# LayerNorm of the first chunk in pairs of blocks, and the first Q and K spreads in more and smaller loads, in a fused attention + gated-MLP kernel

## The chip, the cores and the metric

One core of one Trainium2 chip. The metric is the device time of one execution in microseconds; the kernel before was run five times. A profile of one execution gives the times of the single instructions.

## The reference

For x of 2048 rows and 640 columns, the layer adds attention and a gated MLP, both computed from one LayerNorm, to x:

```python
xn = _layernorm(x, axis=-1)                     # no weight, eps 1e-5
# attention: 32 heads of 20, each row sees itself and the 255 rows before it
qkv = (xn @ wqkv).reshape(1, 2048, 3, 32, 20)
scores = q @ k.T * 20 ** -0.5;  p = softmax(masked scores)
A = (p @ v) @ wo
# gated MLP, hidden width 1536
B = (sigmoid(xn @ w_gate) * (xn @ w_up)) @ w_down
return x + A + B
```

(The lines of attention are put together from the reference's own, batch and transposes left out.)

## The kernel before

The 2048 rows are worked in four chunks of 512, and a chunk in four blocks of 128 rows. For a chunk:

- **LayerNorm.** `ln_block` (L191 to L201) takes the statistics of a block on VectorE (`bn_stats` L195 twice, `bn_aggr` L197) and 1/sqrt on GpSimd (L199, L200, tile `rstd`). `norm_block` (L205) makes `xn` on VectorE. `transpose_block` (L213) turns a block with five TensorE transposes into a PSUM tile `pt`, which ScalarE (chunk 0, L216) or VectorE (later chunks, L218) copies to `xnT`, rows along the free dimension.
- **V.** `proj_v` makes a block's V: ten matmuls (L260) in two halves, each copied out to `v` (L264; on ScalarE for chunk 0). GpSimd first sets the extra columns of `v` (L255, L256).
- **Q and K.** `proj_block` makes a fifth of Q or K of a chunk: five matmuls (L234, tile `pqk`), a cast to `st` (Q on VectorE L238, K on ScalarE L240), and a store of 128 KB from `st` to a scratch in HBM (`sq`, `sk`, L242). `spread` (L249) loads Q or K back from the scratch, so that heads lie at 32-row steps: tile `qT` or `kT`, eight groups of four heads, 128 KB for each group. Each group needs rows of all five stores.
- **Scores and output.** `scores` (L394 matmuls into `ps`, L400 exp on ScalarE to `pT`, L405 and L409 masks on GpSimd) goes in three steps for each group of heads; `pv` (L420) multiplies by V, and `finish_group` (L430 on, VectorE) divides.
- **MLP.** `g_gu`: gate (L319, `pg`), tanh on ScalarE (L322, `th`), up (L326, `pu`), and the product on VectorE (L330, `h`). `down` (L345) and `outp` (L358, L363) finish a block with the output projection and the residual x.

The order on every engine is the order in which the program emits instructions, and that is written out by hand. All loads are issued by SyncE (SP) except x of block 1, which ScalarE issues, and one half of the last block's output. SyncE issues in program order, so a transfer that waits for a store holds up those behind it.

The start runs so: x of chunk 0 in four loads by block, with the V part of the QKV weights in between (L135 to L140), the Q and K parts, the first halves of the gate and up weights (L153), and zeros for the scratch (L149). Then LayerNorm, transposes and V of chunk 0; then Q and K of chunk 0 (`g_qk(0)`), then `load_rest`: the second halves of the gate and up weights, x of chunk 1 (L118, tile `xc`), the zeros of the second scratch, `wd` and `wo`. The order of LayerNorm and V in chunk 0 is the loop at L486:

```python
    stat = {0: ln_block(0, 0)}
    for s in range(SBC + 1):
        if s + 1 < SBC:
            stat[s + 1] = ln_block(0, s + 1)
        if s < SBC:
            norm_block(0, s, *stat[s])
            transpose_block(0, s, True)
        if s:
            proj_v(0, s - 1)
```

After that a loop (L529) emits the steps of `scores` for all chunks and groups and, between them, "fill" work of TensorE, by credit: gate and up of chunk 0 first, six such tiles ahead of the first scores (L525). From the tenth piece of that fill on, LayerNorm of chunk 1 (`g_norms(1)`) is mixed in, so its statistics stand in VectorE's order among the `h` of chunk 0.

PSUM buffers: `pt`, `pv`, `pqk`, `pg`, `pu` share three (`ps_d`); `ps` has two of two banks (`ps_s`), `acc` one. Five buffers of `st`, four of `pT`, two of `th`.

Of the kernel before, what the change touches and what calls it, by code (L numbers as in the profile page):

```python
# [18 lines left out]
SBC = CW // P  # L19
HG = 4  # L20
NG = H // HG
# [49 lines left out]
def kernel(  # L71
# [119 lines left out]
    def ln_block(c, s):  # L191
        xs = xc[c][:, s, :]
        stats = lnp.tile([P, 2, nc.vector.BN_STATS_DIM], FP32, name="stats")
        for a in range(2):
            nc.vector.bn_stats(out=stats[:, a, :], in_=xs[:, a * 320:(a + 1) * 320])  # L195
        mv = lnp.tile([P, nc.vector.BN_AGGR_DIM], FP32, name="mv")
        nc.vector.bn_aggr(out=mv, in_=stats)  # L197
        rstd = lnp.tile([P, 1], FP32, name="rstd")
        nc.gpsimd.tensor_scalar(out=rstd, in0=mv[:, 1:2], scalar1=EPS, scalar2=None, op0=ADD)  # L199
        nc.gpsimd.tensor_tensor(out=rstd, in0=rstd, in1=neghalf, op=POW)  # L200
        return mv, rstd  # L201

    def norm_block(c, s, mv, rstd):
        xn = lnp.tile([P, D], BF16, name="xn", bufs=4)
        nc.vector.tensor_scalar(out=xn, in0=xc[c][:, s, :], scalar1=mv[:, 0:1],  # L205
                                scalar2=rstd[:, 0:1], op0=SUB, op1=MULT)
        xns[c, s] = xn

    def transpose_block(c, s, act):
        xn = xns.pop((c, s))  # L210
        pt = ps_d.tile([P, DC, P], BF16, name="pt", tag="d")
        for d in range(DC):
            nc.tensor.transpose(pt[:, d, :], xn[:, d * P:(d + 1) * P], ident)  # L213
        dst = xnT[c][:, :, s * P:(s + 1) * P]
        if act:
            nc.scalar.copy(out=dst, in_=pt)  # L216
        else:
            nc.vector.tensor_copy(out=dst, in_=pt)  # L218

    def new_xnT(c):  # L220
        xnT[c] = xtp.tile([P, DC, CW], BF16, name="xnT")
# [5 lines left out]
    def proj_block(w, c, m):  # L227


        base = 0 if w == "q" else D  # L230
        ps = ps_d.tile([P, CW], FP32, name="pqk", tag="d")
        for d in range(DC):
            wt = wqkv[:, d, base:base + D].rearrange("p (k m) -> p m k", m=DC)
            nc.tensor.matmul(ps, lhsT=wt[:, m, :], rhs=xnT[c][:, d, :],  # L234
                             start=(d == 0), stop=(d == DC - 1))
        st = stp.tile([P, CW], BF16, name="st")
        if w == "q":
            nc.vector.tensor_copy(out=st, in_=ps)  # L238
        else:
            nc.scalar.copy(out=st, in_=ps)  # L240
        dst = scratch[w, c % 2].rearrange("(h j) s -> h j s", j=32)
        nc.sync.dma_start(out=dst[:, 4 * m:4 * m + 4, :], in_=st)  # L242

    def spread(w, c, g0, g1):

        if g0 == 0:
            qk[w, c] = (qp if w == "q" else kp).tile([P, NG, CW], BF16, name=w + "T")
        src = scratch[w, c % 2].rearrange("(g p) s -> p g s", p=P)
        nc.sync.dma_start(out=qk[w, c][:, g0:g1, :], in_=src[:, g0:g1, :])  # L249

    def proj_v(c, s):
        v = vp.tile([P, H * VW + 11], BF16, name="v")
        vt[c * SBC + s] = v
        v3 = v[:, 0:H * VW].rearrange("p (h d) -> p h d", d=VW)
        nc.gpsimd.memset(v3[:, :, DH:VW], 0.5)  # L255
        nc.gpsimd.memset(v[:, H * VW:], 0.0)  # L256
        for hf in range(2):
            ps = ps_d.tile([P, CW], FP32, name="pv", tag="d")
            for d in range(DC):
                nc.tensor.matmul(ps[:, 0:HALF], lhsT=xnT[c][:, d, s * P:(s + 1) * P],  # L260
                                 rhs=wqkv[:, d, 2 * D + hf * HALF:2 * D + (hf + 1) * HALF],
                                 start=(d == 0), stop=(d == DC - 1))
            copy = nc.vector.tensor_copy if c else nc.scalar.copy
            copy(out=v3[:, hf * 16:(hf + 1) * 16, 0:DH],  # L264
                 in_=ps[:, 0:HALF].rearrange("p (h d) -> p h d", d=DH))
# [24 lines left out]
    def g_qk(c):  # L290
        for w in "qk":
            for m in range(DC):
                proj_block(w, c, m)
                if w == "k" and m == 1:
                    spread("q", c, 0, NG)
                yield 5 * MM
        if c == 0:
            spread("k", c, 0, 1)
            spread("k", c, 1, NG)

    def g_v(c):
        for s in range(SBC):
# [179 lines left out]
            yield cost  # L482

    new_xnT(0)
    stat = {0: ln_block(0, 0)}
    for s in range(SBC + 1):  # L486
        if s + 1 < SBC:
            stat[s + 1] = ln_block(0, s + 1)
        if s < SBC:
            norm_block(0, s, *stat[s])  # L490
            transpose_block(0, s, True)
        if s:
            proj_v(0, s - 1)
    for _ in g_qk(0):
        pass
    load_rest()
# [7 lines left out]

    fill.add("gu0", mix(g_gu(0, 0, 12), chain(g_norms(1), g_transposes(1)), 9), 12 * GU + 1280)
    fill.add("qk1", mix(g_qk(1), g_norms(2), 2), 50 * MM)
    fill.add("v1", g_v(1), 40 * 136)
    fill.add("gu1a", g_gu(1, 0, 1), 1 * GU)
    fill.add("out0", mix(g_out(0), g_transposes(2), 1, 3), OUT + 1280)
    fill.add("x3", later(3), 0)  # L510
    fill.add("qk2", g_qk(2), 50 * MM)
    fill.add("v2", g_v(2), 40 * 136)
    fill.add("gu1b", mix(g_gu(1, 1, 12), g_norms(3), 10), 11 * GU)
# [31 lines left out]
    c = NCH - 1  # L545
# [46 lines left out]
```

## Time and profile before

| | us |
|---|---|
| five runs, median (lowest to highest) | 335.84 (334.18 to 337.28) |
| the profiled execution | 334.18 |
| its span, first to last instruction | 332.4 |
| TensorE matmul busy | 320.0 |
| ScalarE busy | 218.2 |
| GpSimd busy | 165.0 |
| VectorE busy | 163.4 |
| granted TensorE clock | 1.00 |

The profiled execution was the quickest of the five runs. The page says what each engine was busy with; a matmul counts as busy while it streams, and the ends of matmuls are modelled. Where the time goes is read from the stretches in which TensorE is idle: 12.4 us in the span. Of the first 60 us the engines look like this (busy us in the stretch, DMA rate):

| stretch | TensorE | VectorE | ScalarE | GpSimd | DMA GB/s |
|---|---|---|---|---|---|
| 6 to 8 | 0.78 | 1.73 | 0.69 | 1.07 | 370 |
| 8 to 14 (three of 2) | 6.00 | 1.79 | 4.62 | 2.12 | 368 to 372 |
| 30 to 32 | 1.60 | 0.53 | 0.60 | 0.00 | 66 |
| 32 to 34 | 1.46 | 0.39 | 1.09 | 0.00 | 219 |
| 34 to 40 (three of 2) | 6.00 | 1.38 | 5.03 | 2.78 | 373 to 376 |
| 40 to 44 (two of 2) | 2.93 | 0.80 | 2.49 | 0.89 | 364 to 406 |

### The profile page before, as it was taken

The page shows a single profiled execution, that of the slowest core. Times are in us where ns is not written, and L with a number is a line of the kernel's source. Part 1 is how long each engine was busy: PE and PEld are TensorE (multiplying, and loading weights), DVE is VectorE, ACT ScalarE, POOL GpSimd, SP SyncE. Part 2 cuts the span into 40 slices and gives each one's busy share as a digit, 9 for nine tenths or more (in the row PEclk, how much of TensorE's full clock was granted, in tenths as well). Part 3 has the DMA queues.
Part 4 walks back from the last instruction along what each step waited for, and adds up shares of the span by engine and source line. Part 5 has one row for each costly group of instructions (what it writes and reads, how often), then busy time and mean ns, then how long its engine had stood idle before and what let it go on. Part 6 is the DMA issues. An engine that isn't in the chain of part 4 may idle for free.

```text
span 332.4 us, 7219 instructions
## 1 busy us (share of the span) xinstructions
PE 320.0 (96%) x2884; PEld 165.0 (50%) x2884; DVE 163.4 (49%) x333; ACT 218.2 (66%) x274; POOL 165.0 (50%) x312
## 2 busy tenths in 40 slices
PE   7998979989899999999999999999999999999996
PEld 2653323445466655544455654544445664444664
DVE  5232177698654363636954445443443425444142
ACT  2623776769666568788875667868887657878300
POOL 5200457576655554664954455565455554554300
PEclk9999999999999999999999999999999999999999
DMA  8956997125501044700000012630000010000001
GB/s 271 376 183 196 373 390 224 35 81 156 177 0 42 22 130 130 238 17 3 0 2 22 20 41 81 205 128 4 0 2 1 26 37 20 2 0 2 2 17 62
DMA packets 26224, 30.89 MB, mean 93 GB/s; under 512 B 1456, under 2 KB 25648, under 8 KB 26160
## 3 DMA queue, kind: packets, MB, share of 16 engines
q1 hardware_dynamic: 25904, 30.20, 27.5%
q8 instruction: 22, 0.36, 0.5%
q10 hardware_dynamic: 288, 0.25, 0.2%
q14 instruction: 10, 0.08, 0.1%
HBM read 21.00 MB, written 10.26 MB: 94 GB/s over the span
## 4 chain that ended last, share of the span: by engine, by line
PE 84%; DMA 6%; ACT 3%; DVE 3%; POOL 1%; SPq 1%; issue 1%; ACTq 0%; POOLq 0%
PE y L345 16%; PE pqk L234 14%; PE pu L326 13%; PE pg L319 13%; PE ps L394 9%; PE y L358 7%; PE acc L420 6%; PE pv L260 6%; DMA xc<-in_A_x_dram 5%; ACT pT L400 3%; DMA sk<-st 1%; PE pt L213 1%; DVE stats L195 1%; DVE t L430 0%; POOL pT L405 0%
## 5 line engine op out<-in xcount | busy, mean ns | idle before, releaser
L400 ACT ACTIVATE pT<-ps 128x1024 bf16<-128x1024 f32 (+2 forms) x192 | 175.9, 971 | 61.8 <-PE ps L394 58.0
L405 POOL TENSOR_SCALAR_AFFINE_SELECT pT<-pT 128x512 bf16<-128x512 bf16 x128 | 81.7, 638 | 79.8 <-ACT pT L400 79.6
L409 POOL TENSOR_SCALAR_AFFINE_SELECT pT<-pT 128x512 bf16<-128x512 bf16 x112 | 71.8, 641 | 58.1 <-ACT pT L400 58.1
L330 DVE SCALAR_TENSOR_TENSOR h<-th,pu 128x512 bf16<-128x512 f32 x48 | 32.7, 682 | 59.9 <-PE pu L326 21.3
L319 PE MATMUL pg<-xnT,wg 128*128 128x512 bf16 x240 | 59.8, 380 | 1.0 <-DVE h L330 1.0
L326 PE MATMUL pu<-xnT,wu 128*128 128x512 bf16 x240 | 59.9, 380 | 0.0
L345 PE MATMUL y<-wd,h 128*128 128x320 bf16 x384 | 57.3, 300 | 0.0
L234 PE MATMUL pqk<-xnT,wqkv 128*128 128x512 bf16 x200 | 46.6, 381 | 0.0
L394 PE MATMUL ps<-qT,kT 20*128 20x384 bf16 (+2 forms) x704 | 39.6, 275 | 5.2 <-ACT pT L400 4.2
L345 PEld LDWEIGHTS <-h 128*128 128x128 bf16 x384 | 35.7, 98 | 16.8 <-issue 4.0
L322 ACT ACTIVATE th<-pg 128x512 f32<-128x512 f32 x48 | 28.8, 600 | 13.9 <-PE pg L319 13.3
L430 DVE STREAM_TRANSPOSE t<-acc 128x512 f32<-128x512 f32 x32 | 22.8, 713 | 28.5 <-PE acc L420 28.1
L319 PEld LDWEIGHTS <-wg 128*128 128x128 bf16 x240 | 22.1, 98 | 28.3 <-issue 4.5
L326 PEld LDWEIGHTS <-wu 128*128 128x128 bf16 x240 | 21.3, 98 | 27.0 <-issue 5.2
L234 PEld LDWEIGHTS <-wqkv 128*128 128x128 bf16 x200 | 22.3, 119 | 19.3 <-issue 2.9
L363 DVE SCALAR_TENSOR_TENSOR y_sb<-y,xc 128x320 bf16<-128x320 f32 x32 | 15.4, 490 | 32.6 <-PE y L358 32.6
L394 PEld LDWEIGHTS <-kT 20*128 20x128 bf16 x704 | 12.3, 92 | 37.0 <-issue 35.3
L420 PE MATMUL acc<-pT,v 128*32 128x384 bf16 (+2 forms) x704 | 25.7, 277 | 0.2 <-POOL pT L405 0.2
L260 PE MATMUL pv<-wqkv,xnT 128*128 128x320 bf16 x160 | 23.9, 299 | 0.4 <-DVE v L264 0.4
L358 PE MATMUL y<-wo,oc 128*128 128x320 bf16 x160 | 24.1, 299 | 0.0
L420 PEld LDWEIGHTS <-v 128*32 128x32 bf16 x704 | 15.0, 96 | 13.6 <-issue 11.0
L238 DVE CAST st<-pqk 128x512 bf16<-128x512 f32 x20 | 13.8, 688 | 12.5 <-PE pqk L234 10.8
(32 smaller groups left out, 175.4 us busy)
## 6 DMA issues: line engine op xcount, KB each, us to landing
qT<-sq SPq DMA_DIRECT2D x4, 1024.0 KB, 6.0
kT<-sk SPq DMA_DIRECT2D x3, 1024.0 KB, 5.3
sq<-st SPq DMA_DIRECT2D x20, 128.0 KB, 2.2
sk<-st SPq DMA_DIRECT2D x20, 128.0 KB, 3.0
wqkv<-in_A_wqkv_dram SPq DMA_DIRECT2D x3, 800.0 KB, 5.7
out_dram<-y_sb SPq DMA_DIRECT2D x15, 160.0 KB, 1.8
wg<-in_B_w_gate_dram SPq DMA_DIRECT2D x2, 960.0 KB
wu<-in_B_w_up_dram SPq DMA_DIRECT2D x2, 960.0 KB
```

Source lines behind the costliest of these rows:

```text
L234: nc.tensor.matmul(ps, lhsT=wt[:, m, :], rhs=xnT[c][:, d, :], start=(d == 0), stop=(d == DC - 1))
L260: nc.tensor.matmul(ps[:, 0:HALF], lhsT=xnT[c][:, d, s * P:(s + 1) * P], rhs=wqkv[:, d, 2 * D + hf * HALF:2 * D + (hf + 1) * HALF], start=( ...
L319: nc.tensor.matmul(pg, lhsT=part(wg, d, f), rhs=xnT[c][:, d, :], start=(d == 0), stop=(d == DC - 1))
L326: nc.tensor.matmul(pu, lhsT=part(wu, d, f), rhs=xnT[c][:, d, :], start=(d == 0), stop=(d == DC - 1))
L330: nc.vector.scalar_tensor_tensor(out=h, in0=th, scalar=1.0, in1=pu, op0=ADD, op1=MULT)
L345: nc.tensor.matmul(ys[hf], lhsT=ht[c, f][:, s * P:(s + 1) * P], rhs=wd[:, f, hf * HALF:(hf + 1) * HALF], start=(f == 0), stop=False)
L358: nc.tensor.matmul(ys[hf], lhsT=oc[c, m][:, s * P:(s + 1) * P], rhs=wo[:, m, hf * HALF:(hf + 1) * HALF], start=False, stop=(m == DC - 1))
L394: nc.tensor.matmul(pss[i // 2][:, i % 2, col * P:(col + n) * P], lhsT=qk["k", kc][32 * i:32 * i + DH, g, kb * P:(kb + 1) * P], rhs=qk["q", ...
L400: nc.scalar.activation(out=pt[:, 2 * a:2 * a + 2, 0:width * P], in_=pss[a][:, :, 0:width * P], func=EXP, scale=SCALE)
L405: nc.gpsimd.affine_select(out=v, in_=v, pattern=[[0, HG], [1, P]], compare_op=GE, fill=0.0, base=0, channel_multiplier=-1)
L409: nc.gpsimd.affine_select(out=v, in_=v, pattern=[[0, HG], [-1, P]], compare_op=GE, fill=0.0, base=-1, channel_multiplier=1)
L420: nc.tensor.matmul(acc[32 * i:32 * i + 32, q0 * P:(q0 + n) * P], lhsT=v[:, h * VW:h * VW + 32], rhs=pt[:, i, col * P:(col + n) * P], start ...
```

## The change

LayerNorm of chunk 0 goes in two pairs: statistics of two blocks, then normalisation and transposes of both, then V of both. The load of Q of chunk 0, which was one of 1,024 KB, becomes one of groups 0 and 1 (256 KB) at the same place and one of groups 2 to 7 (768 KB) behind K's second load. The load of K, which was group 0 (128 KB) and groups 1 to 7 (896 KB), becomes group 0, groups 1 and 2 (256 KB) and, behind the second of Q, groups 3 to 7 (640 KB). Later chunks are as before. Lines from L301 on move down by two.

```diff
             for m in range(DC):
                 proj_block(w, c, m)
                 if w == "k" and m == 1:
-                    spread("q", c, 0, NG)
+                    spread("q", c, 0, NG if c else 2)
                 yield 5 * MM
         if c == 0:
             spread("k", c, 0, 1)
-            spread("k", c, 1, NG)
+            spread("k", c, 1, 3)
+            spread("q", c, 2, NG)
+            spread("k", c, 3, NG)
...
     new_xnT(0)
-    stat = {0: ln_block(0, 0)}
-    for s in range(SBC + 1):
-        if s + 1 < SBC:
-            stat[s + 1] = ln_block(0, s + 1)
-        if s < SBC:
-            norm_block(0, s, *stat[s])
+    for s0 in range(0, SBC, 2):
+        stat = [ln_block(0, s) for s in (s0, s0 + 1)]
+        for s in (s0, s0 + 1):
+            norm_block(0, s, *stat[s - s0])
             transpose_block(0, s, True)
-        if s:
-            proj_v(0, s - 1)
+        for s in (s0, s0 + 1):
+            proj_v(0, s)
     for _ in g_qk(0):
         pass
     load_rest()
```

## The prediction

> **What bounds the kernel now.** I read the chain that ended last first, then its pieces in order of time over the first 60 us, where all of the change lies.
>
> ```profile
> PE 84%; DMA 6%; ACT 3%; DVE 3%; POOL 1%; SPq 1%; issue 1%; ACTq 0%; POOLq 0%
> PE y L345 16%; PE pqk L234 14%; PE pu L326 13%; PE pg L319 13%; PE ps L394 9%; PE y L358 7%; PE acc L420 6%; PE pv L260 6%; DMA xc<-in_A_x_dram 5%; ACT pT L400 3%; DMA sk<-st 1%; PE pt L213 1%; DVE stats L195 1%; DVE t L430 0%; POOL pT L405 0%
> ```
>
> TensorE carries the span: 320.0 us busy of 332.4, so 12.4 us idle in all, and no edit that leaves the matmuls alone can win more. The transfers in the chain are two: the loads of x, 5%, and the stores of K, 1%. The pieces of the chain say where:
>
> ```profile
> 14.33 10.81 PE pqk L234 x50
> 25.16 0.59 ACT st L240
> 25.77 4.51 DMA sk<-st
> ...
> 30.75 0.44 SPq L249
> 31.23 0.56 SPq L153
> 31.83 0.53 SPq L153
> 32.41 10.78 DMA xc<-in_A_x_dram
> 43.20 0.90 DVE stats L195 x2
> 44.34 0.76 DVE stats L195 x2
> 45.25 0.64 DVE h L330
> ```
>
> Columns: start and length in us, then what. The path does not run through the first scores. It goes from the last store of K (25.77, landed 30.28) through SyncE's queue (the K loads, gate and up weights) to the load of x of chunk 1, which lands at 43.2; LayerNorm of chunk 1 stands ahead of an h in VectorE's order, and TensorE then needs that h. The list of waits over the span and over 30 to 56 us prices the stops (total, times, longest, us):
>
> ```profile
> PE pt L213 <- DVE xn L205: 1.2, 1, 1.2
> PE ps L394 <- DMA kT<-sk: 0.9, 1, 0.9
> PE pg L319 <- DVE h L330: 1.0, 2, 0.7
> DVE stats L195 <- DMA xc<-in_A_x_dram: 4.3, 1, 4.3
> ```
>
> The change aims at the first two rows. The timeline shows that the last two stand behind them: the h of 45.25 us is for a pu whose matmuls began at 39.40; it waits behind the statistics, and pg at 45.94 needs its PSUM buffer.
>
> **What the Trainium skill says.** "DMA: Bandwidth & Descriptors", Anatomy of one DMA, puts a fixed 2.0 us on each transfer, most of it the receipt of the last write. The trace agrees: Q stores of the later chunks land in 2.0 us (minimum and median). The same page, Two DMAs through the same engine are not ordered, has a dependent load wait for the completion of the store; SyncE's issue of the K load waits up to 3.7 us here. Specifications there give 358 to 368 GB/s; here 34 to 43 us moved 376. "SBUF — State Buffer", Who interferes with whom, says that VectorE in a two-port mode and GpSimd block each other. The trace fits: xn takes 394 to 450 ns, but 646 ns at 9.95 us, amid GpSimd's memsets of v.
>
> **Part 1, LayerNorm in pairs.** No instruction is added. Four orders change.
> VectorE: xn of block 1 goes ahead of the statistics of block 2 (6.39 to 7.44). It now waits for rstd, ready at 6.84. GpSimd's four memsets of v of blocks 0 and 1 stand right behind that rstd, so xn takes 0.39 to 0.65 and ends at 7.25 to 7.5. T1, the five transposes, starts at 7.29 to 7.55 instead of 7.89: 0.34 to 0.60 of the 1.2 us wait goes.
> TensorE: before, T0 T1 V0 T2 V1 T3 V2 V3 (V: a block's ten V matmuls); after, T0 T1 V0 V1 T2 T3 V2 V3. V1 used to cover the copy of block 2 to xnT on ScalarE; now only T3 does. T1 at 7.55, V0 0.29 later, V0 and V1 2.72 (four halves of 0.68), so T2 at 10.55 and TensorE free at 11.12. The copy begins about 0.5 after T2's start (9.54 to 10.06 before), behind V1's last 0.43 us eviction, and takes 0.70: V2 at 11.8, a new stall of 0.68. V2 and V3 end 2.72 later, at 14.52, against 14.17 before, when pqk L234 began. With the quick xn: 14.26. So this part costs 0.09 to 0.35; I take **+0.2**.
> xn of block 3 comes at about 10.5 to 11.1: T3 can slip a few tenths inside the stall. GpSimd's memsets pass ahead of rstd of blocks 2 and 3, which wait for statistics anyway; ScalarE's evictions of V1 pass ahead of that copy, counted above. All of it shifts K's last store, and so x of chunk 1, by as much.
>
> **Part 2, smaller loads.** SyncE issues two more L249 loads, at 0.34 to 0.44 each: 0.8 us ahead of the gate weights. In the stretch 23.6 to 26.3 (KB each, median us to landing), with a later chunk's Q stores (minimum, median, maximum) below:
>
> ```profile
> qT<-sq SPq DMA_DIRECT2D x1, 1024.0 KB, 6.0
> sk<-st SPq DMA_DIRECT2D x3, 128.0 KB, 5.3
> ...
> DMA to landing us min/median/max: 2.0/2.0/3.6
> ```
>
> The Q load (issued 23.28, landed 29.3) stands ahead of the last three K stores, whose last took 4.51 instead of 2 to 3. With 256 KB in place of 1,024, 768 KB (786 kB) leave the way, 2.3 us at 26 to 28 us' 340 GB/s. The last store then lands about 1.0 after that Q load, as before, or 2.0 to 3.0 after issue: 28.0 to 28.8, taken 28.3. K's first load is issued 2.0 us earlier and takes 2.15 (30.36 to 32.5 before): 30.5. First scores follow the gate and up matmuls that end at 31.6, so the **0.94 us wait goes**. 0.2 from part 1 leaves that unchanged. Groups 0 and 1 have Q and K by about 31.5; group 1's scores ran at 39.1. The rest of both lands by about 36; group 2's scores ran at 47.1. No wait is added at TensorE.
>
> But the 768 KB of Q and the K loads stand ahead of x of chunk 1, and that queue is full:
>
> ```profile
> 30.00:31.00 1.00, 1.00 (x6) 0.42 (x5) 0.24 (x1) 0.44 (x1) 0.00 (x0) 1.00 0.00 0
> 34.00:43.00 9.00, 7.94 (x63) 3.17 (x61) 1.38 (x2) 6.99 (x12) 3.67 (x6) 1.00 1.07 376
> ```
>
> The last two columns are DMA share and GB/s: empty at 30, saturated from 34 to 43. Starting 2.05 earlier and carrying 786 kB more at 376 GB/s (2.09) cancel: x lands at 43.2 + 0.05, plus part 1's 0.2. Unknown is the ramp after an issue (2 to 3 us below full rate here): bounds -0.6, if short loads in flight together fill it, and +2.1, if the store lands no earlier. SyncE's issues have room: x's would come at 31 to 32, before at 32.41. The counters of completion, reused in turn every eight transfers, now make the second gate load wait for the first Q load and a K clear for K's first load: both landed by then.
>
> TensorE thus arrives about 0.75 us earlier at the pg that waits for h, and h still waits for x: the 0.36 us stop there grows to about 1.1, and what follows starts where it did, plus x's delay. **Late next is x of chunk 1.**
>
> **Sum.** Part 1 +0.2; K wait -0.94, given back at h +0.94; x +0.05, rounded with the two transfers' own gaps to +0.1. Total +0.3 on the profiled execution's 334.18 (span 332.4). That execution was the quickest of five, 1.66 below their median; on 335.84 this gives **336.1**.
>
> **Rivals.** A, the gain is kept: x lands 0.9 or more earlier, because the half-empty stretches (144 GB/s at 24 to 26, 0 at 30, 66 at 30 to 32) are filled. Net -0.94 + 0.2 = -0.7: 335.1. For it: that empty microsecond. Against: in the new order the same stretch still only waits for K's store. For more than 1% (3.4 us), nearly all waits of TensorE before 56 us (1.2 + 0.9 + 1.4 at ScalarE's exp + 1.0 at h) would have to vanish.
> B, slower: K's last store keeps its 4.5 us since writing, not the Q load, holds it. Then K's first load is no earlier, the 0.94 stays, and x waits behind 786 kB more: +2.1 + 0.2, **338.1**. It decides from the point where the store gains less than 2.1 us. For it: the first Q store, with no Q load ahead, took 3.9. Against: that one followed the clears, and all three K stores landed just after Q. Past 1% it needs x 3.4 us late, so further contention.
> C, the split does nothing because scores wait for the whole tile: before, the first scores began 1.8 us after the issue of the 896 KB K load, which needs 2.4 at 376 GB/s, so they wait for their own piece. That leaves little for C.
>
> **How the numbers follow.** Forecast 0.60, A 0.16, B 0.19, others (C and shifts of later stages) 0.05. 1% is about what a measurement of this kernel tells from no change (its runs span 334.18 to 337.28). The forecast itself lies within 1%, A mostly and B too, B with a tail beyond: faster 0.07, same 0.80, slower 0.13. The range takes in A's 335.1 less a microsecond of run spread and B's 338.1 with half of one: 334.1 to 338.6.
>
> **What would show it.** Part 1: T1 near 7.4, a gap of about 0.6 before V2, pqk at 14.2 to 14.5. Part 2: K's last store landing at 28 to 29, no wait of ps for K. Absorption: x landing at 43 to 44, VectorE's wait there still above 3 us, pg's wait on h grown. x at 42 or earlier speaks for A, at 45 for B. The forecast is wrong if x comes late and TensorE does not mind, or if later stages shift by more than a microsecond.

## The result, and the profile after

The changed kernel takes 334.76 us in the median of 44 runs (333.84 to 336.62); the kernel before, run again beside it, 335.27 (333.95 to 339.95, 79 runs). The ratio is 0.9973, interval 0.9958 to 0.9989: 0.27% faster. The lowest runs differ by 0.1 us; the highest by 3.3. The ratios leave out executions more than 1.5% above the fastest; the ranges here do not.

The profiled execution took 335.24, its span is 333.4, TensorE is busy for 321.6 and its mean granted clock is 0.995. So this execution is longer than the profiled one before (334.18), though the kernel is not slower. The path of the changed kernel by engine, and the pieces of it that answer to those shown before (start, length, us):

```profile
PE 85%; DMA 5%; ACT 3%; DVE 3%; SPq 1%; POOL 1%; issue 1%; ACTq 0%
```

```profile
26.04 2.04 DMA sk<-st
...
32.15 11.23 DMA xc<-in_A_x_dram
...
43.40 0.90 DVE stats L195 x2
```

K's last store lands after 2.04 us instead of 4.51, yet x of chunk 1 lands at 43.4, as before (43.2). TensorE's waits (total, times, longest):

```profile
PE acc L422 <- POOL pT L411: 2.0, 1, 2.0
...
PE pt L213 <- DVE xn L205: 0.3, 1, 0.3
PE pv L260 <- ACT xnT L216: 0.3, 1, 0.3
PE acc L422 <- POOL pT L407: 0.3, 1, 0.3
```

The wait for K's load and the wait of pg for h are gone, that of T1 is down from 1.2 to 0.3 in this execution, and one of 2.0 us is new: the P·V matmuls of head group 1 wait for a mask of GpSimd, which stands behind LayerNorm of chunk 1. What follows it in the timeline of TensorE, and in one-microsecond stretches (stretch; length; busy us of TensorE, weight loads, VectorE, ScalarE, GpSimd; clock; DMA share; GB/s):

```profile
50.84 0.41 PE L422 MATMUL acc<-pT,v 128*32 128x384 bf16 x4 [1.98 <-POOL pT L411]
...
52.08 2.31 PE L328 MATMUL pu<-xnT,wu 128*128 128x512 bf16 x5
```

```profile
51.00:52.00 1.00, 0.74 (x12) 0.22 (x7) 1.00 (x3) 0.00 (x0) 0.92 (x3) 0.50 0.48 205
52.00:53.00 1.00, 1.00 (x7) 0.38 (x4) 0.93 (x3) 0.46 (x1) 1.00 (x3) 0.50 0.82 307
53.00:54.00 1.00, 1.00 (x4) 0.20 (x2) 0.97 (x2) 0.63 (x2) 0.83 (x2) 0.50 0.75 222
```

After 1.98 us without a matmul, TensorE's clock is at half, and five matmuls that take 1.25 us elsewhere take 2.31. This explains most of the 1.0 us between the two spans; the other 0.2 is x of chunk 1, which landed at 43.40 and not at 43.20. It turned the question from where the time went to **what differs between runs of one kernel**.

### The profile page after: what moved, and what is told of

Same layout as the page of the kernel before. It is cut to its first block, busy times and chain, and to the rows that moved or that the text cites. A ratio compares the mean times of both kernels' runs of the same rounds, so it can differ in the third digit from the quotient of the medians.

```text
span 333.4 us, 7220 instructions
## 1 busy us (share of the span) xinstructions
PE 321.6 (96%) x2884; PEld 165.4 (50%) x2884; DVE 163.6 (49%) x333; ACT 218.3 (65%) x274; POOL 164.9 (49%) x312
## 4 chain that ended last, share of the span: by engine, by line
PE 85%; DMA 5%; ACT 3%; DVE 3%; SPq 1%; POOL 1%; issue 1%; ACTq 0%
PE y L347 15%; PE pu L328 14%; PE pqk L234 14%; PE pg L321 13%; PE ps L396 9%; PE y L360 7%; PE acc L422 7%; PE pv L260 6%; DMA xc<-in_A_x_dram 4%; ACT pT L402 3%; DVE stats L195 1%; PE pt L213 1%; DMA sk<-st 1%; SPq L153 1%; SPq L249 1%
## 5 line engine op out<-in xcount | busy, mean ns | idle before, releaser
L328 PE MATMUL pu<-xnT,wu 128*128 128x512 bf16 x240 | 61.0, 385 | 0.0
L324 ACT ACTIVATE th<-pg 128x512 f32<-128x512 f32 x48 | 28.8, 600 | 13.6 <-PE pg L321 11.8
```

The lines of the kernel that those rows point to most:

```text
L328: nc.tensor.matmul(pu, lhsT=part(wu, d, f), rhs=xnT[c][:, d, :], start=(d == 0), stop=(d == DC - 1))
```

## The experiments

Full clock below means a mean granted clock of 0.998 or more. Beside the first four, 34 of 59 runs of the kernel before were at full clock (334.11 to 335.33); the rest reached 340.23.

| kernel | median (range), us | runs at full clock | ratio [interval] |
|---|---|---|---|
| changed, again | 335.07 (334.01 to 336.48) | 11 of 22 | 0.9975 [0.9954, 0.9996] |
| pairs alone | 335.07 (334.52 to 336.10) | 22 of 22 | 0.9975 [0.9956, 0.9995] |
| small loads alone | 335.18 (333.95 to 340.02) | 11 of 22 | 0.9993 [0.9968, 1.0018] |
| changed, x of chunk 1 first | 331.99 (331.86 to 332.09) | 6 of 6 | 0.9878 [0.9836, 0.9920] |
| before, x of blocks 2, 3 first | 336.86 (334.65 to 339.49) | 9 of 22 | 1.0043 [1.0020, 1.0066] |
| pairs, x of chunk 1 first | 333.13 (332.85 to 333.50) | 11 of 11 | 0.9926 [0.9898, 0.9953] |
| before, four filler matmuls | 334.95 (334.18 to 336.50) | 22 of 22 | 0.9991 [0.9971, 1.0012] |
| small loads, both x first | 333.86 (331.73 to 336.23) | 9 of 22 | 0.9947 [0.9925, 0.9969] |
| before, xn of block 1 early | 335.14 (334.76 to 336.44) | 14 of 14 | 0.9989 [0.9969, 1.0009] |
| changed, x of chunk 1 first, V split | 332.01 (331.87 to 332.15) | 6 of 6 | 0.9896 [0.9873, 0.9919] |

**The changed kernel again.**

> The changed kernel once more, beside its parts. Every theory: ratio to the kernel before 0.996 to 0.999, as measured. Theory 1 (the gain at the first scores is given back where TensorE meets work that waits for x of chunk 1): in a profile at full clock the span is within 0.3 us of 332.4, x lands at 43 to 44, and TensorE waits 1.5 to 2.5 us more than before between 40 and 52 us. Theory 3 (the gain is kept): span 331.7 or less.

The profiled execution is one at full clock: 334.01, span 332.2. Its wait for the mask, the five matmuls behind it, and the stretch that showed the half clock above:

```profile
PE acc L422 <- POOL pT L411: 1.6, 1, 1.6
```

```profile
51.53 1.25 PE L328 MATMUL pu<-xnT,wu 128*128 128x512 bf16 x5
```

```profile
51.00:52.00 1.00, 0.87 (x11) 0.44 (x11) 1.00 (x3) 0.00 (x0) 0.92 (x4) 1.00 0.48 205
52.00:53.00 1.00, 1.00 (x6) 0.26 (x5) 0.90 (x4) 1.00 (x2) 1.00 (x2) 1.00 0.75 282
```

The same kernel: x landed at 43.03 instead of 43.40, the wait was 1.61 instead of 1.98, the clock stayed at 1.00. The median of the 11 runs at full clock is 334.46, of the other 11 335.33. The span is 0.2 below that of the profile before, though no wait for K's load is left: most of the gain at the first scores is given back, as theory 1 has it. The waits that take it back are smaller than the 1.5 to 2.5 us expected: 1.93 us at the two masks, against 1.25 at h and the mask before.

**The two halves alone.**

```diff
 # pairs alone: the loop of the change; loads as before
 # small loads alone: the spread() lines of the change; loop as before
```

> LayerNorm in pairs alone, loads as before. Theory 1: pqk begins 0.1 to 0.35 us later than the 14.17 of before, the wait for K's load stays at about 0.9, x lands 0.1 to 0.35 later; ratio 1.000 to 1.001. Theory 2 (the pairs bring the gain): ratio 0.997. Theory 4 (the kernel before has a long upper tail of runs, and the tail comes from K's load): highest run still above 338.

> The smaller loads alone, LayerNorm order as before. Theory 1: no wait for K's load, last K store lands about 28, x of chunk 1 at 43.0 to 43.4; ratio 0.998 to 1.000. Theory 2: 1.000. Theory 3: ratio 0.996 to 0.997, span about 331.5. Theory 4: highest run below 337.

Theory 4 falls, and the other way round: the pairs cut the upper tail, the small loads do not. At full clock the pairs cost 0.29 us (medians 335.07 against 334.78 of before) and the small loads win 0.49 (334.29). Theory 2 has the right kernel for the wrong reason: the pairs' order is slower, but all 22 runs lie within 1.6 us. In one point theory 1 missed: in the profile of the pairs alone K's last store took longer than in the profile before, so the wait for K's load grew to 1.4 and x of chunk 1 landed 0.96 later, not 0.1 to 0.35:

```profile
26.23 5.03 DMA sk<-st
...
44.16 0.90 DVE stats L195 x2
```

The profile of the small loads alone fell on a long execution, 337.73. VectorE and TensorE at its start:

```profile
7.11 0.89 DVE L195 BATCH_NORM_STATS2 stats<-xc 128x6 f32<-128x320 bf16 x2 [0.89 <-DMA xc<-in_A_x_dram]
```

```profile
6.28 0.45 PE L213 MATMUL pt<-ident,xn 128*128 128x128 bf16 x5
8.60 0.45 PE L213 MATMUL pt<-ident,xn 128*128 128x128 bf16 x5 [1.87 <-DVE xn L205]
8.89 2.65 PE L260 MATMUL pv<-wqkv,xnT 128*128 128x320 bf16 x10
```

x of block 2 of chunk 0 landed at 7.1, against 6.4 in the profile before. The statistics that wait for it stand ahead of xn of block 1, so T1 waited 1.87 us and not 1.23. Then V of block 0 took 2.65 instead of the 1.52 before:

```profile
8.18 1.52 PE L260 MATMUL pv<-wqkv,xnT 128*128 128x320 bf16 x10
```

In the kernel with the small loads alone the clock was at half there:

```profile
9.00:10.00 1.00, 1.00 (x6) 0.55 (x4) 0.86 (x3) 0.69 (x1) 0.77 (x4) 0.56 1.07 365
10.00:11.00 1.00, 1.00 (x5) 0.61 (x4) 0.34 (x1) 0.43 (x1) 0.94 (x7) 0.50 1.07 366
```

This execution had a second fall at 53 us, behind a wait of 1.87 for the mask. "TensorE: Matmul & The Clock Gate", Part 1 of the Trainium skill, describes this: the array's clock is halved after an idle window of some 3.4 us and comes back after 3.4 busy. The runs agree on the half and on the return (about 3.4 us at 0.5 in the changed kernel); they do not agree that it takes 3.4 us of idling: 1.87 and 1.98 were enough. What decides is worked out in the last section.

**Is it the wait before T1?** Three edits of the kernel before.

```diff
 # before, four filler matmuls
             transpose_block(0, s, True)
+        if s == 0:
+            ps = ps_d.tile([P, CW], FP32, name="pwarm", tag="d")
+            for k in range(4):
+                nc.tensor.matmul(ps, lhsT=warm[:, 0:P], rhs=warm, start=(k == 0), stop=(k == 3))
 # before, xn of block 1 early: its norm_block ahead of ln_block(0, 2), TensorE's order as before
 # (the lines that keep these calls from coming twice are left out)
+        if s == 0:
+            stat[1] = ln_block(0, 1)
+            norm_block(0, 0, *stat[0])
+            norm_block(0, 1, *stat[1])
 # before, x of blocks 2, 3 first
-    load_wqkv(2)
     for s in (2, 3):
         nc.sync.dma_start(out=xc[0][:, s, :], in_=xr[:, s, :])
+    load_wqkv(2)
```

> The kernel before with four more matmuls of the warm-up kind (0.86 us, their result unused) between the first and the second block's transposes. Theory C (a TensorE wait of about 1.9 us makes the granted clock fall to half for some 3 us, and part of the tail is that): the wait is shortened to 1.0 to 1.3 even where x is late, the clock stays at 1.0 in nearly all runs, highest run at 337 or below, median 334.6. If the tail is the late load alone: highest still above 338, with the clock at 1.0.

The filler's matmuls compute nothing that is used. With them TensorE is idle for only 0.45 us before T1 in the profile:

```profile
6.70 1.03 PE L495 MATMUL pwarm<-st 128*128 128x512 bf16 x4
8.18 0.45 PE L213 MATMUL pt<-ident,xn 128*128 128x128 bf16 x5 [0.45 <-DVE xn L205]
```

T1 is even later than before (8.18; x of block 2 at 6.7), but no run's clock fell below 0.998, and the highest is 336.50 where the kernel before reached 339.99 beside it. Theory C holds for the tail: a good part of it is the clock, not the lateness. The rest, the 2.3 us from lowest to highest run, remains with the clock full. The median, 334.95, is not the 334.6 expected, and the ratio does not exclude 1. No long execution of the kernel before was profiled; that its clock falls at T1 follows from this edit and the next, and from the pairs.

> The kernel before with one change, on VectorE alone: xn of block 1 ahead of the statistics of block 2 (TensorE's order T0 T1 V0 T2 V1 T3 V2 V3 as before, loads as before). Theory A (the first transposes of block 1 must not wait for the load of x of block 2): the tail goes as with the pairs, highest run below 336.6, clock at 1.0 in nearly all runs; T1 at 7.3 to 7.6, V0 then ends ahead of xn of block 2, a new wait of about 0.8 before T2, pqk at 14.2 to 14.6; median 334.6 to 335.1, ratio 0.996 to 0.998. Theory B (TensorE's new order or ScalarE's takes the tail away): tail up to 338 or more, ratio 1.000.

All 14 runs at full clock, none above 336.44, with one order on VectorE changed: theory A holds for the clock. Beside it 9 of 19 runs of the kernel before were below full clock. The expected new wait is there, and eats the gain:

```profile
7.62 0.45 PE L213 MATMUL pt<-ident,xn 128*128 128x128 bf16 x5 [0.72 <-DVE xn L205]
...
10.11 0.45 PE L213 MATMUL pt<-ident,xn 128*128 128x128 bf16 x5 [0.67 <-DVE xn L205]
```

pqk begins at 14.75, later than the 14.2 to 14.6 expected, and the ratio, 0.9989 where 0.996 to 0.998 was expected, does not exclude 1.

> The kernel before, with only the loads of x of blocks 2 and 3 of chunk 0 moved ahead of the load of the V weights. Theory A (the pairs gain because the first transposes of block 1 no longer wait, behind the statistics of block 2, for a load that is sometimes late): with that load early the upper tail goes; highest run below 336.5 where the kernel before reaches 338 to 340, ratio 0.993 to 0.997; T1 at 7.3 to 7.5. Theory B (the pairs gain by their order on TensorE or ScalarE): no change, 1.000, tail as before.

A miss: 1.84 us slower in the median than the kernel before beside it. x came early, but the V weights, now behind it, landed at 9.65, 7.5 us after their issue, and V of block 0 waited for them. The wait was only moved, and it halves the clock too (ten matmuls of V in 2.83 us):

```profile
9.79 2.83 PE L260 MATMUL pv<-wqkv,xnT 128*128 128x320 bf16 x10 [1.76 <-DMA wqkv<-in_A_wqkv_dram]
```

So this edit can't speak on x of block 2.

**Is the gain of the small loads given back at x of chunk 1?**

```diff
     def load_rest():
+        load_x(1)
         for k in range(1, F // FS):
             load_gu(k)
-        load_x(1)
```

> The changed kernel with the load of x of chunk 1 ahead of the second halves of the gate and up weights. Theory 1: x lands at 37 to 39, VectorE waits for it under 1 us, TensorE's waits between 40 and 52 us fall by 1 us or more; ratio 0.992 to 0.996. If the late gate weights (about 43 instead of 38) hold TensorE instead, 1.000. Theory 3: no different from the changed kernel, 0.997.

> LayerNorm in pairs and the load of x of chunk 1 ahead of the second gate and up weights, but the old loads of Q and K. Theory 1 (what the small loads win at the first scores is kept once x is no longer late): slower than the 331.99 of the kernel with both by 0.9 to 1.4 us, so 332.9 to 333.4, ratio 0.990 to 0.993; a wait for K's load of 0.9 to 1.5 us in the profile. If the small loads do nothing even so: 332.0.

331.99 with the small loads, 333.13 without: 1.14 us, in the range that theory 1 gave. The two were measured at different times; beside them the kernel before took 335.11 and 335.02. VectorE of the kernel with both, where 5.23 us of waiting for x stood in the changed kernel, and TensorE's wait in the one with the old loads:

```profile
37.69 0.69 DVE L332 SCALAR_TENSOR_TENSOR h<-th,pu 128x512 bf16<-128x512 f32 x1 [2.28 <-PE pu L328]
38.30 0.88 DVE L195 BATCH_NORM_STATS2 stats<-xc 128x6 f32<-128x320 bf16 x2
```

```profile
PE ps L394 <- DMA kT<-sk: 1.4, 1, 1.4
```

The statistics start without a wait behind the h before them, and the wait of 2.0 us for the mask is gone. What the small loads win at the first scores now reaches the end. All runs of the two lie within 0.3 and 0.7 us, all at full clock, and no TensorE wait in their profiles is above 1.4 once the first matmuls have run. The ratio of the kernel with both, 0.9878, is below the 0.992 to 0.996 expected. Moving one line is worth 3.1 us on the changed kernel, more than the change itself, and the gate weights, 640 KB later, hold up nothing.

**Two tries for more.**

> The old LayerNorm order with x of blocks 2 and 3 loaded ahead of the V weights, the small loads of Q and K, and x of chunk 1 ahead of the second gate and up weights. Theory A and theory 1 together: no tail, TensorE's wait before T1 about 0.7, no stall before V of block 2, pqk at 13.6 to 14.2 instead of 14.4 to 14.8; 331.0 to 331.7, ratio 0.985 to 0.988. If x of chunk 0 still comes late in some runs, a tail up to 336.

> The changed kernel with x of chunk 1 ahead of the second gate and up weights, and the transposes of block 2 between the two halves of V of block 1. The stall of 0.6 to 0.7 before V of block 2 shrinks to 0.1 to 0.3, so pqk begins 0.3 to 0.5 earlier than the 14.6 of that kernel without the split, and the time falls as much: 331.5 to 331.8, ratio 0.986 to 0.988. If xn of block 2 or 3 comes too late for it: 332.0 again.

Both miss. The first has the late V weights of above: its lowest run is the lowest of all, 331.73, but more than half of its runs lose clock. The profiled one did not, though V waited as long:

```profile
9.88 1.52 PE L260 MATMUL pv<-wqkv,xnT 128*128 128x320 bf16 x10 [1.75 <-DMA wqkv<-in_A_wqkv_dram]
```

In the second, splitting V of block 1 removed the stall before V of block 2, but T3 now waits 0.39 for xn of block 3, and V of block 2 starts at 11.78 instead of 11.92: 332.01. The best version found is the changed kernel with x of chunk 1 first; V split is no different from it.

## Why the prediction was wrong

The forecast was 336.1, a loss of 0.3 us; measured was a gain of 0.27%. Beside one another the mean of all runs is 0.75 us lower with the change (335.03 against 335.77), at full clock 0.22. The larger part thus lies in the runs that lose clock: before, 25 of 59, with a median 1.9 us above that at full clock; after, 11 of 22, but only 0.9 above. Measured against the profiles, the parts of the forecast:

**Pairs, at full clock: right, to 0.15 us.** T1 at 7.26 to 7.64 in the profiles of the four kernels with the pairs and V in whole blocks (7.29 to 7.55 forecast), V of block 2 at 11.71 to 11.92 (11.8), pqk at 14.44 to 14.65 (14.26 to 14.52). Cost 0.29 in the medians; forecast 0.2.

**K's store and the first scores: right.** Landing at 28.08 (28.3), no wait for K's load. Worth 1.14 once nothing takes it back; 0.94 forecast. The section that the prediction names for the fixed 2.0 us is about transfers that GpSimd issues, and those here are SyncE's; the sum rests on the 2.0 us that the trace shows.

**x of chunk 1 takes the gain back: the mechanism is right, the place is not.** In six profiles in which LayerNorm of chunk 1 waits for x and the clock is full from then on, the span ends the same time after x lands, whatever TensorE won before:

| profile | x of chunk 1 lands | span | difference |
|---|---|---|---|
| before | 43.20 | 332.45 | 289.2 |
| changed, again | 43.03 | 332.21 | 289.2 |
| pairs alone | 44.16 | 333.42 | 289.3 |
| before, four filler matmuls | 43.67 | 332.91 | 289.2 |
| before, xn of block 1 early | 44.42 | 333.66 | 289.2 |
| before, x of blocks 2, 3 first | 46.95 | 336.20 | 289.3 |

The place failed: "TensorE thus arrives about 0.75 us earlier at the pg that waits for h". No pg waits for h any more:

```profile
45.94 1.24 PE L319 MATMUL pg<-xnT,wg 128*128 128x512 bf16 x5 [0.36 <-DVE h L330]
```

```profile
44.69 1.24 PE L321 MATMUL pg<-xnT,wg 128*128 128x512 bf16 x5
45.44 0.64 DVE h L332
```

Before (first line), pg starts when h is done; in the changed kernel (the other two) it starts ahead of that h. In the trace its matmuls wait on a semaphore of ScalarE and no longer of VectorE, so the changed program gives this pg another PSUM buffer. The small loads alone bring that, the pairs alone do not. TensorE runs on and stops at the mask, for 1.6 to 2.0 us in one piece. I had not compared these buffers. In one piece the wait is dear: the profiled execution lost clock there, and half of the runs lose it somewhere. The kernel with x of chunk 1 first has the old buffers again, so its 3.1 us include what the new ones cost; the 1.14 us does not, as both of its kernels have the old ones.

**The step that failed is the last of the sum:** "That execution was the quickest of five, 1.66 below their median; on 335.84 this gives 336.1." This carries a difference worked out on one execution over to the median, as if the 1.66 were spread that the change can't touch. Both halves of the change touch it.

- *The clock, which the sum leaves out.* The pairs alone, the filler and the early xn each shorten the wait before T1, and none of their 58 runs loses clock. I priced that wait at the 1.2 us that the quickest execution shows; with x of block 2 later by 0.7 it is 1.87, and the clock falls on top.
- *The store of K.* At full clock, too, the kernel before has a median of 334.78, 0.6 above its profile. K's last store, behind the large Q load, took 4.51 us in that profile, the least of six profiles with the old loads (up to 5.03); behind the small one it took 2.04 to 2.05 in three. So the term for x was right against that one profile, and mis-sized against the others. In the changed kernel x lands 0.17 earlier to 0.20 later than in that profile; 0.25 later was forecast. But the median spans at full clock are 333.05 before, 332.4 with the small loads, 333.3 with the pairs and 332.5 with both. By the table above the small loads then bring x forward by 0.65 to 0.8 us (an estimate), where I had 0.05 later. Of this, 0.5 to 0.6 arrives in the medians of the time.
- *Luck.* The five runs had a median of 335.84; the 79 runs have 335.27.

That edge was not in the view that I used, but a spread of 334.18 to 337.28 for a profile taken at the bottom of it should have been a question.

**Rivals.** A, the gain is kept, forecast 335.1 and is nearest in number. In part it is what happens at full clock, with x earlier by less than its 0.9; in full it is what x first makes of the change. B is refuted: the store landed in 2.04. C as well: the first scores start at 31.80 without a wait, when less than 1 MB of the 1.8 MB of loads up to K's last piece has moved.

So at full clock the change gains 0.3 us (334.46 against 334.78): the pairs cost 0.29 and the small loads win 0.6 on top of them. In the other runs the pairs remove the fall of the clock that the late T1 brings, and the small loads bring a cheaper one, in the profile behind the mask. The two effects of the small loads cancel: beside it, the kernel with the pairs alone has the same median, 335.07.

Open: why the buffers were given otherwise; where the other runs of the changed kernel lose their clock; the rest of the spread at full clock; and why the time outside the span is 1.9 us with the small loads and 1.7 before. That the fall at 51 us costs the microsecond rests on the comparison of executions (its span ends 290.0 after x lands, not 289.2 or 289.3); no edit took that wait alone away.

## What to carry to other kernels

A profile is one execution: where its time lies at the edge of the runs', ask which wait is longest in the others, and look for loads that stand ahead of TensorE's first work on an in-order engine. A TensorE wait of just under 2 us can cost half its length again in clock, and waits that fall into the same 3.4 us add up. A gain at a stage is kept only if the next wait comes later for another reason; find that one, and move its load first.

## What the runs showed of the hardware

In these traces the clock falls on a grid of time. In the four falls on record it stayed at half for 3.41 us, and each fall came a whole number of times 3.41 us after the clock had first reached full: 13 times in the changed kernel (6.62 to 50.99), once and 14 times in the small loads alone (5.70 to 9.11 and to 53.49), once with x of blocks 2, 3 first (5.76 to 9.18). The start of this grid differs from profile to profile, 4.04 to 7.28. What decides is how long TensorE was idle in all within such a stretch:

| profile | stretch of 3.41 us from | TensorE idle in it | clock after it |
|---|---|---|---|
| small loads alone | 50.07 | 2.17 | half |
| before, x of blocks 2, 3 first | 5.76 | 2.04 | half |
| changed | 47.58 | 1.98 | half |
| small loads alone | 5.70 | 1.96 | half |
| small loads, both x first | 7.81 | 1.75 | full |
| small loads, both x first | 4.40 | 1.67 | full |

No other stretch of the twelve profiles, up to 325 us, has more than 1.63, and none was followed by a fall. So the edge lies between 1.75 and 1.96 us, a little over half of the stretch. This settles what the length of one wait does not: the wait of 1.76 us shared its stretch with another of 0.90, and the clock fell 0.6 us before it ended; the one of 1.75 stood alone; that of 1.61 in the changed kernel was cut in two by the grid, 0.91 and 0.70. It also lets the same kernel lose clock in some runs and not in others; that the start of the grid decides there is not shown, as those runs left no trace. A fall costs about 1 us.
